# One load per weight, halves joined by fp32 products, and an earlier hidden layer in a decode kernel

The kernel runs on one core of a Trainium2 chip. The metric is device microseconds of one execution; quoted times are medians of several runs, and a ratio is the mean time of one kernel's fast runs over the mean of the other's fast runs in the same rounds, so it is not quite the ratio of the quoted medians. A run is called slow when it is over 1.5% above the fastest of the same kernel. Spans in a profile are about 1.8 us shorter than the time of the same run.

## The reference

Two blocks on the same normalized token, for a batch of 2: attention of one query over the last 2048 keys, and a feed-forward layer with squared ReLU; both are added to the input.

```python
xn = _layernorm(x)                                # x: 2 x 1 x 576
q = (xn @ wq)                                     # wq: 576 x 4096, 32 query heads of 128
scores = einsum("bhqd,bhkd->bhqk", q, k) * 128**-0.5    # 16 kv heads, 2048 keys
o = einsum("bhqk,bhkd->bhqd", softmax(scores), v)
A = o.reshape(B, 1, 4096) @ wo                    # wo: 4096 x 576
h = xn @ w1 + b1                                  # w1: 576 x 4608
B = relu(h)**2 @ w2 + b2                          # w2: 4608 x 576
return x + A + B
```

## The kernel before

The work on K and V is cut into 8 units u (4 kv heads of one sample), 2 MB of K and 2 MB of V each. `step(u)` transposes K of unit u, multiplies it with q, takes the softmax, and in its gaps multiplies the probabilities of unit u-2 with V. The loads stand in one queue in program order. These are the parts that the change touches:

```python
# weights: 4 whole rows per partition (512 of the 576 rows) in two loads, the remaining 64 rows in a third
def issue_w(tiles, wt, i, name, width, lrem):
    if i < NFULL // RW:
        tl = wbig.tile([P, RW * WBW], BF16, tag="wbig", name=f"{name}_{i}")        # two buffers
        ...
    else:
        tl = wrem.tile([P, WRW], BF16, tag="wrem", name=f"{name}_rem")
...
def pv_sum(u):                # sum of exp over partitions: one fp32 product with a 128x128 weight
    if u % (2 * B) == 0:
        sm_tiles[tq // 2] = psum.tile([P, B * Dh + 2 * B], F32, tag="sm", ...)       # one bank
    rs = sm_tiles[tq // 2][:, B * Dh + u % (2 * B):...]
    pe_mm(rs, lhsT=samec[:]..., rhs=sum_tiles.pop(u)[:], start=True, stop=True, ...)
    nc.vector.reciprocal(out=ri[:], in_=rs)
    nc.vector.tensor_scalar(out=f[:], in0=own_j[:], scalar1=ri[:, 0:1], ...)         # factors of o
...
def mlp_h_end():              # squared ReLU on rows, then nine bf16 transposes of every ninth column
    ...
    for r in range(FR):
        pe_tr(out=ha[:, r, 0:RB], in_=hrow[:, r:HW:FR], identity=ident[0:RB, 0:RB])
...
load_k(1); load_v(0); load_k(2); load_v(1); load_k(3)
...
step(1)
for u in range(2, NU - 1):
    step(u)
    ...
    if u == 4:
        issue_wo(0)
        for i in range(NW): issue_w1(i)           # w1 is loaded in the middle
    ...
pv_out(NU - 4); pv_all(NU - 3); wo_acc(0)
for c in range(KC): mlp_h_block(c)                # hidden layer in the tail, piece by piece
mlp_h_end()
pv_out(NU - 3)
step(NU - 1, with_pv=False)
pv_all(NU - 2); pv_out(NU - 2); pv_all(NU - 1); pv_out(NU - 1)
wo_acc(1)
for w in W2P[:NG4 - 1]: mlp_o(*w)                 # products with w2
```

Of the kernel before, what the change touches and what calls it, by code (L numbers as in the profile page):

```python
# [8 lines left out]
F32 = mybir.dt.float32  # L9
# [7 lines left out]
def kernel(  # L17
# [15 lines left out]
    P = 128  # L33
# [23 lines left out]
    NFULL = D // P  # L57
    RW = 2
    REM = D - NFULL * P
    S = P // REM  # L60
    KC = NFULL + 1
    NXN = NFULL + S
    LQ = (Hq * Dh) // S
    L1 = F // S
    NG4 = 4
    QW = Hq * Dh // NG4
    QB = QW // 2
    QH = QW // Dh
# [3 lines left out]
    RB = 32 * (NG4 - 1) + B  # L72
# [9 lines left out]
    wbig = ctx.enter_context(tc.tile_pool(name="wbig", bufs=NFULL // RW))  # L82
    wrem = ctx.enter_context(tc.tile_pool(name="wrem", bufs=1))
# [14 lines left out]
    k_tiles, v_tiles, wq_tiles, w1_tiles, wo_tiles, w2_tiles = {}, {}, {}, {}, {}, {}  # L98
    WBW = max(Hq * Dh, F)
    WRW = max(LQ, L1)  # L100
# [13 lines left out]
    def issue_w(tiles, wt, i, name, width, lrem):  # L114
        if i < NFULL // RW:
            tl = wbig.tile([P, RW * WBW], BF16, tag="wbig", name=f"{name}_{i}")
            rows = wt[0:NFULL * P, :].rearrange("(p r) n -> p (r n)", r=NFULL)
            nc.sync.dma_start(out=tl[:, 0:RW * width], in_=rows[:, i * RW * width:(i + 1) * RW * width])  # L118
            for r in range(RW):
                tiles[i * RW + r] = tl[:, r * width:(r + 1) * width]  # L120
        else:
            tl = wrem.tile([P, WRW], BF16, tag="wrem", name=f"{name}_rem")
            nc.sync.dma_start(out=tl[:, 0:lrem], in_=wt[NFULL * P:D, :].rearrange("r (s l) -> (r s) l", s=S))  # L123
            tiles[NFULL] = tl

    def issue_wq(c):
        issue_w(wq_tiles, A_wq, c, "wq", Hq * Dh, LQ)

    def issue_w1(c):
        issue_w(w1_tiles, B_w1, c, "w1", F, L1)  # L130

    def w_rows(tiles, c, col0, n, L):
        if c < NFULL:
            return tiles[c][:, col0:col0 + n], c
        sg = col0 // L
        assert (col0 + n - 1) // L == sg
        return tiles[c][:, col0 - sg * L:col0 - sg * L + n], NFULL + sg
# [20 lines left out]
    x_sb = const.tile([B, D], BF16, name="x_sb")  # L158
    nc.scalar.dma_start(out=x_sb[:], in_=x2d)
# [6 lines left out]
    NW = NFULL // RW + 1  # L166
    for i in range(NW):
        issue_wq(i)
    ones_f = const.tile([P, P], F32, name="ones_f")
    nc.vector.memset(ones_f[:], 1.0)  # L170
    col_f = const.tile([P, P], F32, name="col_f")
# [12 lines left out]
    ones_b = const.tile([1, B], BF16, name="ones_b")  # L184
    nc.vector.memset(ones_b[:], 1.0)
# [3 lines left out]
    for i in range(2):  # L189
        nc.vector.bn_stats(out=stats[:, i, :], in_=x_sb[:, i * half_d:(i + 1) * half_d])  # L190
# [6 lines left out]
    xn_sb = const.tile([B, D], BF16, name="xn_sb")  # L197
    nc.vector.tensor_scalar(out=xn_sb[:], in0=x_sb[:], scalar1=mv[:, 0:1], scalar2=rstd[:, 0:1],  # L198
                            op0=ALU.subtract, op1=ALU.mult)
    xr_sb = const.tile([B, S, P], BF16, name="xr_sb")  # L200
    nc.vector.memset(xr_sb[:], 0.0)
    for sg in range(S):
        nc.vector.tensor_copy(out=xr_sb[:, sg, sg::S], in_=xn_sb[:, NFULL * P:D])

    pro_ps = psum.tile([P, NXN, B], BF16, tag="misc", name="pro_ps")
    for c in range(NFULL):
        pe_tr(out=pro_ps[:, c, :], in_=xn_sb[:, c:NFULL * P:NFULL], identity=ident[:B, :B])
    for sg in range(S):
        pe_tr(out=pro_ps[:, NFULL + sg, :], in_=xr_sb[:, sg, :], identity=ident[:B, :B])
    xnT = const.tile([P, NXN, B], BF16, name="xnT")  # L210
    nc.vector.tensor_copy(out=xnT[:], in_=pro_ps[:])
# [21 lines left out]
    samec = const.tile([P, P // NC, NC], F32, name="samec")  # L233
    nc.gpsimd.tensor_copy(out=samec[:], in_=own[:].unsqueeze(1).to_broadcast([P, P // NC, NC]))
    tohead = const.tile([P, NC, DW], F32, name="tohead")
    nc.gpsimd.tensor_copy(out=tohead[:], in_=own[:].unsqueeze(2).to_broadcast([P, NC, DW]))
    qz = const.tile([P, 2, NU, 2, 4, NC], BF16, name="qz")
# [16 lines left out]
    def q_block(c):  # L254
        for k in range(2):
            for g in range(NG4):
                rhs, xc = w_rows(wq_tiles, c, g * QW + k * QB, QB, LQ)
                pe_mm(q_ps[k][32 * g:32 * g + B, :], lhsT=xnT[:, xc, :], rhs=rhs,
                                 start=(c == 0), stop=(c == KC - 1), skip_group_check=True,
                                 tile_position=(0, 32 * g))  # L260
        if c == KC - 1:
            qrow = const.tile([RB, QW], BF16, tag="row", name="qrow")
            nc.vector.tensor_copy(out=qrow[:, 0:QB], in_=q_ps[0][0:RB, :])
            nc.scalar.copy(out=qrow[:, QB:QW], in_=q_ps[1][0:RB, :])
            qT_ps = psum.tile([P, QH, P], BF16, tag="misc", name="qT_ps")
            for i in range(QH):
                pe_tr(out=qT_ps[:, i, 0:RB], in_=qrow[:, i * Dh:(i + 1) * Dh],
                                    identity=ident[0:RB, 0:RB])
            qT_v = qT_ps[:].rearrange("p i (g s) -> p i g s", s=32)
            for b in range(B):  # L270
                nc.vector.tensor_copy(out=qT_all[:, b, :].rearrange("p (g i) -> p i g", g=NG4), in_=qT_v[:, :, :, b])
            qe_ps = psum.tile([P, 2 * NU, NC], F32, tag="sm", name="qe_ps")
            for e in range(2):
                pe_mm(qe_ps[:, e * NU:(e + 1) * NU, :], lhsT=par[:, e, :, :].rearrange("p a i -> p (a i)"),
                                 rhs=qT_all[:].rearrange("p b h -> p (b h)"), start=True, stop=True)
            for a, cp in ((0, nc.vector.tensor_copy), (1, nc.scalar.copy)):
                lo, hi = a * (P // 2), (a + 1) * (P // 2)
                for w in range(2):
                    cp(out=qz[lo:hi, :, :, w, 2 * w + a, :].rearrange("p e u c -> p (e u) c"), in_=qe_ps[lo:hi, :, :])

    kT_tiles, sc_tiles, pT_tiles, sum_tiles, sm_tiles = {}, {}, {}, {}, {}
# [34 lines left out]
    def softmax(u):  # L316
# [12 lines left out]
        sums = keep.tile([P, 1], F32, tag="sums", name=f"sums_{u}")  # L329
        nc.scalar.activation(out=pr[:], in_=sc_ps, func=ACT.Exp, bias=nb[:], scale=scale, accum_out=sums[:])  # L330
        pT = keep.tile([P, NT, 32], BF16, tag="pT", name=f"pT_{u}")
        nc.vector.transpose(out=pT[:].rearrange("p t m -> p (t m)"), in_=pr[:])  # L332
        pT_tiles[u], sum_tiles[u] = pT, sums
# [3 lines left out]
    def pv_sum(u):  # L337
        tq, b = divmod(u, B)
        if u % (2 * B) == 0:
            sm_tiles[tq // 2] = psum.tile([P, B * Dh + 2 * B], F32, tag="sm", name=f"sm_{tq // 2}")  # L340
        rs = sm_tiles[tq // 2][:, B * Dh + u % (2 * B):B * Dh + u % (2 * B) + 1]
        pe_mm(rs, lhsT=samec[:].rearrange("p x c -> p (x c)"), rhs=sum_tiles.pop(u)[:],
                         start=True, stop=True, skip_group_check=True)
        f = work.tile([P, 4], F32, tag="f", name=f"f_{u}")
        ri = work.tile([P, 1], F32, tag="ri", name=f"ri_{u}")
        nc.vector.reciprocal(out=ri[:], in_=rs)
        nc.vector.tensor_scalar(out=f[:], in0=own_j[:], scalar1=ri[:, 0:1], scalar2=None, op0=ALU.mult)
        pv_cur[u] = (psum.tile([P, 4, Dh], F32, tag="misc", name=f"pv_ps_{u}"), f)

    def pv(u, i):  # L350
        pv_ps, f = pv_cur[u]
        v = v_tiles[u][:].rearrange("p (w t x) -> p t w x", w=2, t=NT)
        for k in range(4):
            t = 4 * i + k
            pe_mm(pv_ps[32 * k:32 * (k + 1), :, :].rearrange("m (w a) d -> m w (a d)", w=2),
                                  lhsT=pT_tiles[u][:, t, :], rhs=v[:, t, :, :], start=(i == 0),
                                  stop=(i == NT // 4 - 1), skip_group_check=True, tile_position=(0, 32 * k))

    def pv_mix(u):
        pv_ps, f = pv_cur[u]  # L360
        acc = None
        for j in range(4):
            nx = work.tile([P, Dh], F32, tag=f"acc{j % 2}", name=f"acc_{u}_{j}")
            if j == 0:
                op = nc.vector.tensor_scalar(out=nx[:], in0=pv_ps[:, j, :], scalar1=f[:, j:j + 1], scalar2=None,
                                             op0=ALU.mult)
            else:
                op = nc.vector.scalar_tensor_tensor(out=nx[:], in0=pv_ps[:, j, :], scalar=f[:, j:j + 1], in1=acc[:],  # L368
                                                    op0=ALU.mult, op1=ALU.add)
            tc.keep_in_program_order(op)  # L370
            acc = nx
        pv_cur[u] = acc
# [4 lines left out]
    def pv_out(u):  # L377
        tq, b = divmod(u, B)
        t, half = divmod(tq, 2)
# [204 lines left out]
```

## Time and profile before

| | before |
|---|---|
| median time | 134.56 us (134.39 to 134.71, 4 runs) |
| span of the profiled run | 132.7 us |
| TensorE busy; its granted clock, as a share of full clock | 90.6 us; 0.896 |
| last transfer packet ends | 128.9 us |

The page's head, its transfer row and the end of the timeline are in the prediction below. Further lines of the timeline of the kernel before (columns: start, duration, engine, line, operation, output and inputs, shapes, count, and in brackets the idle time ahead and what ended it):

```profile
35.09 1.09 PE L93 MATMUL kT_ps<-ident_f,k 128*128 128x128 f32 x8 [1.48 <-DMA k<-in_A_k_cache_dram]
...
78.39 0.58 PE L90 MATMUL sm<-sums,samec 128*128 128x1 f32 x2 [2.77 <-DVE od L386]
...
96.75 0.66 PE L90 MATMUL h_ps<-w_rem,xnT 128*2 128x384 bf16 x12 [0.22 <-DMA w_rem<-in_B_w_dram]
99.45 0.74 PE L93 MATMUL ha_ps<-ident,hrow 98*128 98x98 bf16 x9 [2.04 <-DVE hrow L421]
101.82 4.55 PE L93 MATMUL kT_ps<-ident_f,k 128*128 128x128 f32 x24 [1.27 <-DMA k<-in_A_k_cache_dram]
...
122.32 2.37 PE L90 MATMUL out_ps<-w,hT_sb 128*2 128x288 bf16 x36
126.20 1.27 PE L90 MATMUL out_ps<-w,hT_sb 128*2 128x288 bf16 x18 [1.51 <-DMA w<-in_B_w_dram]
```

Step 2 starts when K2 lands (35.1), step 7 when K7 lands (101.8), and the products with w2 wait for w2 (126.2). At each of these places TensorE waits for a transfer, so lateness that arose in between is forgiven. Of the waits that are not for a transfer, one is 2.8 us at 78 us, where the softmax sum of a new half needs the one bank (a part of the memory that TensorE writes) that `od` still has to read.

### The profile page before, as it was taken

To read this page: it belongs to the slowest core of one execution; us is meant where nothing else is said; L and a number is where in the kernel's file an instruction comes from. 1 tells how busy PE (TensorE), PEld (TensorE's weight loads), DVE (VectorE), ACT (ScalarE), POOL (GpSimd) and SP (SyncE) were. 2 spreads that over 40 slices of the span, in tenths; PEclk is the share of its full clock that TensorE was granted. 3 is DMA by queue.
4 is the path that set the end of the run, shared out by engine and by line. 5 is a ranking of instruction groups with operands and counts; after the bars stand their busy time and mean duration, and the time that the engine had idled before them with its cause. 6 is when DMAs were issued, how large, how long until landed. Compare 5 with 4: busy or idle time off the path is not lost.

```text
span 132.7 us, 2075 instructions
## 1 busy us (share of the span) xinstructions
PE 90.6 (68%) x846; PEld 54.2 (41%) x846; DVE 61.5 (46%) x169; ACT 46.2 (35%) x63; POOL 7.3 (6%) x20
## 2 busy tenths in 40 slices
PE   0059645986599689688788639959736974549561
PEld 0059312553356355454444325526315931225330
DVE  6914404264552872873763772277141447540021
ACT  6705502196343274175175133332040752000001
POOL 7500000100100100100100100001000001000000
PEclk9999995599959999999999975799998699855999
DMA  4999999999999999999999999999999999999950
GB/s 154 400 403 444 420 440 430 435 430 415 442 420 435 425 435 425 430 439 425 439 420 444 417 432 422 438 444 439 412 420 425 435 433 433 413 428 433 415 210 1
DMA packets 4260, 53.74 MB, mean 405 GB/s; under 512 B 530, under 2 KB 536, under 8 KB 1052
## 3 DMA queue, kind: packets, MB, share of 16 engines
q1 hardware_dynamic: 4180, 53.61, 95.1%
q8 instruction: 6, 0.10, 0.3%
q0 software_dynamic: 64, 0.01, 0.0%
q14 instruction: 2, 0.02, 0.0%
q10 hardware_dynamic: 8, 0.00, 0.0%
HBM read 53.62 MB, written 0.00 MB: 404 GB/s over the span
## 4 chain that ended last, share of the span: by engine, by line
DMA 73%; PE 13%; SPq 4%; DVE 3%; issue 2%; ACT 2%; POOL 1%; ACTq 0%; POOLq 0%
DMA w_rem<-in_B_w_dram 26%; DMA w<-in_B_w_dram 24%; DMA k<-in_A_k_cache_dram 23%; PE kT_ps L93 8%; PE pv_ps L90 2%; PE sc_ps L90 2%; SPq L118 1%; ACT kT L297 1%; SPq L111 1%; DVE kT L299 1%; DVE mx L319 1%; PE tail_ps L90 1%; POOL gmax L323 1%; SPq L142 0%; SPq L123 0%
## 5 line engine op out<-in xcount | busy, mean ns | idle before, releaser
L93 PE MATMUL kT_ps<-ident_f,k 128*128 128x128 f32 x256 | 43.3, 318 | 7.0 <-DMA k<-in_A_k_cache_dram 4.9
L297 ACT COPY kT<-kT_ps 128x1024 bf16<-128x1024 bf16 x32 | 31.8, 1012 | 31.7 <-PE kT_ps L93 31.6
L93 PEld LDWEIGHTS kT_ps<-ident_f,k 128*128 128x128 f32 x256 | 33.4, 163 | 20.2 <-issue 7.6
L299 DVE COPY kT<-kT_ps 128x1024 bf16<-128x1024 bf16 x32 | 21.9, 685 | 30.8 <-PE kT_ps L93 30.8
L90 PE MATMUL sc_ps<-kT,qz 128*32 128x512 bf16 x128 | 10.5, 413 | 6.5 <-DVE kT L299 5.5
L330 ACT ACTIVATE pr<-sc_ps,nb 128x512 bf16<-128x512 f32 x8 | 5.5, 687 | 20.3 <-DVE nb L327 20.3
L90 PE MATMUL pv_ps<-v,pT 128*32 128x512 bf16 x128 | 12.4, 428 | 0.0
L323 POOL PARTITION_ALL_REDUCE gmax<-m x8 | 2.9, 364 | 102.1 <-DVE m L321 81.2
L368 DVE SCALAR_TENSOR_TENSOR acc<-pv_ps,f,acc 128x128 f32<-128x128 f32 x24 | 8.3, 346 | 0.5
L332 DVE STREAM_TRANSPOSE pT<-pr 128x512 bf16<-128x512 bf16 x8 | 5.7, 709 | 4.8 <-ACT pr L330 4.8
L90 PE MATMUL sm<-acc,tohead 128*64 128x128 f32 x16 | 3.7, 315 | 5.7 <-DVE acc L368 5.5
L319 DVE TENSOR_REDUCE mx<-sc_ps 128x1 f32<-128x512 f32 x8 | 5.5, 691 | 4.2 <-PE sc_ps L90 3.8
L90 PE MATMUL out_ps<-wo,ws 128*2 128x288 bf16 x64 | 5.9, 356 | 1.1 <-DVE ws L390 1.1
L90 PEld LDWEIGHTS <-qz 128*32 128x32 bf16 x128 | 2.2, 98 | 10.8 <-DVE kT L299 7.1
L552 ACT CAST fin_sb<-tail_ps 2x144 bf16<-2x144 f32 x2 | 0.5, 272 | 17.5 <-PE tail_ps L90 17.4
L90 PE MATMUL sm<-sums,samec 128*128 128x1 f32 x16 | 3.2, 267 | 2.8 <-DVE od L386 2.8
L90 PEld LDWEIGHTS <-xnT 128*2 128x2 bf16 x100 | 2.4, 82 | 6.5 <-issue 5.0
L541 DVE COPY part<-out_ps 2x288 f32<-2x288 f32 x2 | 0.9, 448 | 8.9 <-PE out_ps L90 8.9
L90 PEld LDWEIGHTS sm<-acc,tohead 128*64 128x64 f32 x16 | 1.6, 143 | 8.1 <-DVE acc L368 7.5
L93 PE MATMUL pro_ps<-ident,xn_sb 2*128 2x2 bf16 x4 | 0.3, 172 | 6.7 <-DVE xn_sb L198 6.7
L90 PEld LDWEIGHTS <-ws 128*2 128x2 bf16 x64 | 3.3, 102 | 3.8 <-DVE ws L390 1.5
L90 PEld LDWEIGHTS <-pT 128*32 128x32 bf16 x128 | 3.1, 95 | 4.1 <-issue 3.3
(86 smaller groups left out, 64.1 us busy)
## 6 DMA issues: line engine op xcount, KB each, us to landing
k<-in_A_k_cache_dram SPq DMA_DIRECT2D x8, 2048.0 KB, 21.8
v<-in_A_v_cache_dram SPq DMA_DIRECT2D x8, 2048.0 KB, 26.6
wo<-in_A_wo_dram SPq DMA_DIRECT2D x2, 2304.0 KB, 23.4
w<-in_B_w_dram SPq DMA_DIRECT2D x2, 2304.0 KB, 30.9
wq<-in_A_wq_dram SPq DMA_DIRECT2D x2, 2048.0 KB, 13.8
w<-in_B_w_dram SPq DMA_DIRECT2D x3, 1296.0 KB, 28.7
w<-in_B_w_dram SPq DMA_DIRECT2D x1, 1008.0 KB, 31.8
w_rem<-in_B_w_dram SPq DMA_DIRECT2D x1, 576.0 KB, 34.3
```

The costliest lines, as they stand in the source:

```text
L90: return tc.keep_in_program_order(nc.tensor.matmul(out, **kw))
L93: return tc.keep_in_program_order(nc.tensor.transpose(**kw))
L111: return [lambda i=i: nc.sync.dma_start(out=tl[:, i * n:(i + 1) * n], in_=v[:, :, i * n:(i + 1) * n]) for i in range(parts)]
L118: nc.sync.dma_start(out=tl[:, 0:RW * width], in_=rows[:, i * RW * width:(i + 1) * RW * width])
L297: nc.scalar.copy(out=dst, in_=src)
L299: nc.vector.tensor_copy(out=dst, in_=src)
L319: nc.vector.tensor_reduce(out=mx[:], in_=sc_ps, axis=AX.X, op=ALU.max)
L323: nc.gpsimd.partition_all_reduce(gmax[:], m2[:], channels=P, reduce_op=ReduceOp.max)
L330: nc.scalar.activation(out=pr[:], in_=sc_ps, func=ACT.Exp, bias=nb[:], scale=scale, accum_out=sums[:])
L332: nc.vector.transpose(out=pT[:].rearrange("p t m -> p (t m)"), in_=pr[:])
L368: op = nc.vector.scalar_tensor_tensor(out=nx[:], in0=pv_ps[:, j, :], scalar=f[:, j:j + 1], in1=acc[:], op0=ALU.mult, op1=ALU.add)
L541: nc.vector.tensor_copy(out=part[:, i * OH:(i + 1) * OH], in_=out_ps[32 * i:32 * i + B, :])
```

## The change

Each of wq and w1 is to come as one load with 4.5 rows, that is nine half rows, in every partition. A half row can be the left or the right half of a weight row, so a product yields four rows (two samples, two halves), and the halves that belong together are added by a product with a 0/1 selector, in fp32 so that the halves are not rounded to bf16 first. w1 is loaded ahead of K2 and its products stand between steps 1 and 2, so that the tail is relieved. The sum of exp rides as a 129th column in the o product.

```diff
-    wbig = ctx.enter_context(tc.tile_pool(name="wbig", bufs=NFULL // RW))
-    wrem = ctx.enter_context(tc.tile_pool(name="wrem", bufs=1))
+    wbig = ctx.enter_context(tc.tile_pool(name="wbig", bufs=1))
...
+    def issue_w(wt, name, width):
+        tl = wbig.tile([P, HP * FL], BF16, tag="wbig", name=f"{name}_sb")
+        nc.sync.dma_start(out=tl[:, 0:HP * width], in_=wt.rearrange("d (s l) -> (d s) l", s=2)
+                          .rearrange("(p r) l -> p (r l)", r=HP))
...
-        sums = keep.tile([P, 1], F32, tag="sums", name=f"sums_{u}")
+        acc = keep.tile([P, Dh + 1], F32, tag="acc", bufs=4, name=f"acc_{u}")
...                      # pv_sum (a product, a reciprocal, a scaling per unit) goes
-                         lhsT=tohead[:]..., rhs=pv_cur.pop(u)[:], ...
+                         lhsT=tohead[:]..., rhs=acc_tiles.pop(u)[:], ...     # 129 columns
...
     def mlp_h_end():
-        ...pe_tr(out=ha[:, r, 0:RB], in_=hrow[:, r:HW:FR], identity=ident[0:RB, 0:RB])
+        hrow = const.tile([RB, HW], F32, tag="row", name="hrow")
+        for k in range(3):
+            nc.scalar.copy(out=hrow[:, k * HB:(k + 1) * HB], in_=mlp["ps"][k][0:RB, :])
+        for r in range(FR):
+            pe_mm(hT_ps[:, r, :], lhsT=hrow[:, r:HW:FR], rhs=sel_h[0:RB, :, :]..., start=True, stop=True)
...
     load_v(0)
+    issue_w(B_w1, "w1", FL)
     load_k(2)
...
     step(1)
+    mlp_h_start()
+    mlp_h_all()
+    mlp_h_end()
     load_k(4)
...
-    for c in range(KC):
-        mlp_h_block(c)
-    mlp_h_end()
```

The same is done for q, and b1 and b2 are loaded from ACT's queue.

## The prediction

> **What bounds the kernel now.** I read the page's head and its slices first, to see which resource is full and when; then the table of DMA queues, then the stretches of a few microseconds, then the order of the loads on their queue, then the timeline of the last six microseconds.
>
> ```profile
> span 132.7 us, 2075 instructions
> DMA  4999999999999999999999999999999999999950
> GB/s 154 400 403 444 420 440 430 435 430 415 442 420 435 425 435 425 430 439 425 439 420 444 417 432 422 438 444 439 412 420 425 435 433 433 413 428 433 415 210 1
> q1 hardware_dynamic: 4180, 53.61, 95.1%
> DMA 73%; PE 13%; SPq 4%; DVE 3%; issue 2%; ACT 2%; POOL 1%; ACTq 0%; POOLq 0%
> ```
>
> The row DMA is 9 from the second slice to the 38th: the sixteen transfer engines have no hole. One queue moves 53.61 MB and its packets fill 95.1% of 132.7 us, that is 126.2 us per engine. The chain that ended last is 73% transfer. PE, the busiest compute engine, is at 68%. In the stretches (columns: busy times, granted clock, DMA share, GB/s):
>
> ```profile
> 26.00:76.00 50.00, 40.37 (x334) 23.66 (x332) 28.78 (x72) 24.55 (x32) 2.19 (x6) 0.96 1.01 430
> 76.00:96.00 20.00, 15.01 (x154) 8.29 (x158) 9.35 (x24) 5.41 (x8) 0.36 (x1) 0.83 1.00 427
> 110.00:126.00 16.00, 9.36 (x106) 4.82 (x105) 5.75 (x19) 0.78 (x2) 0.36 (x1) 0.79 1.00 424
> ```
>
> The share is 1.00 or more wherever I cut: K and V (first row), wo and w1 (second), w2 (third). So the time is about 2.1 us before the first packet, 126 to 127 us of uninterrupted packets, and a tail. The tail, from the timeline:
>
> ```profile
> 127.50 0.93 DVE L541 COPY part<-out_ps 2x288 f32<-2x288 f32 x2 [8.86 <-PE out_ps L90]
> 128.64 0.61 PE L90 MATMUL tail_ps<-w,hT_sb 128*2 128x144 bf16 x28 [1.17 <-DMA w<-in_B_w_dram]
> 129.53 0.29 PE L90 MATMUL tail_ps<-w,hT_sb 128*2 128x144 bf16 x8
> 130.50 0.33 SPq L553 DMA_DIRECT2D out_dram<-fin_sb  x1
> ```
>
> The last products wait for w2, and 4.1 us follow. Nothing in the change touches that code.
>
> The trace's packet records give a price list. Medians: 16,384 bytes 611 ns, 18,432 bytes 686, 10,368 bytes 389, 8,064 bytes 305, 4,608 bytes 178, 4,096 bytes 159, 2,304 bytes 93; a completion write 9 ns. From 16,384 and 4,096: (611 - 159)/12,288 = 0.0368 ns a byte, 27.2 GB/s per engine or 435 GB/s for sixteen, and 159 - 151 = 8.4 ns fixed per packet. The first packet of K0 starts at 2.13 us, the last of w2 ends at 128.9.
>
> **What the skill says.** The Trainium skill, "DMA: Bandwidth & Descriptors", section "Where 436 GB/s comes from", puts the ceiling of sixteen ports at 435.2 GB/s: the trace agrees, its slope is 435 and its plateau 424 to 431. The same page, "Why small descriptors are slow (HBM only)", has a fixed overhead per packet of about 3 cycles, with examples near 256 bytes; the trace shows 8.4 ns, 1.4% of a 16 KB packet. The same page, "Issuing engines are not separate DMA queues", says loads from another engine's queue save only issue time; in this trace SP's queue carries all but a few KB, so moving b1 and b2 to ACT buys no bandwidth. "TensorE: Matmul & The Clock Gate", Part 1, has TensorE at half clock after about 3.4 us without work; the trace agrees, granted 0.50 at 20 to 26 us after the wait for wq. I use it where the new block of products follows a wait.
>
> **The change, part by part.**
>
> Bytes: unchanged, 53.6 MB.
>
> Packets. K, V, wo and w2 are untouched. wq was 256 packets of 16,384 and 128 of 4,096; on one engine, 16 x 611 + 8 x 159 = 11.05 us. Now 128 rows of 9 x 2048 x 2 = 36,864 bytes; if each is one packet (18,432 bytes are one packet now), the estimate is 8 x (36,864 x 0.0368 + 8.4) = 10.92. w1 was 16 x 686 + 8 x 178 = 12.40; now 8 rows of 41,472 bytes, estimate 8 x (1,526 + 8.4) = 12.28. Four loads fewer save four completion writes, 0.04. Sum: 0.13 + 0.12 + 0.04 = **0.3 us off every transfer engine**, all of it on the path that sets the end.
>
> Start. ACT issues four small loads more behind x, at 0.54 us each as x's issue took: its Sqrt, the layernorm and the first transposes come some 2 us later (xnT was written at 7.2). But wq lands only at about 19 us and K0's transposes have from 8.5 until then, with 5.4 us of work; PE sits idle from 15.8 to 18.0 today. Hidden. K0's own issue is first on SP as before: 0 to 0.1 us.
>
> q. Today the last product comes 0.65 us after the last piece of wq. Now all 36 products wait for the one load: 36 x 64 ns (16 took 1.03 us) = 2.3 us, 4.6 at half clock. Eight fp32 products replace eight transposes (0.83 us); an fp32 product is about 0.2 us each in the pair sm<-acc,tohead (2 in 0.43), so 1.6 us. Scores of unit 0 start 2.5 to 5 us later than 23.1. This is in the shade of transfers.
>
> MLP. With 4.90 us for a 2 MB load, the transfer times are: K0 to 7.0, wq to 18.0, K1 22.9, V0 27.8, w1 40.0, K2 44.9, V1 49.8, K3 54.7, V2 59.6, K4 64.5. w1 in hand at about 41, 54 products at 49 ns (24 took 1.15 us) are 2.6 us, 5.3 at half clock; copies of h by ACT about 1.4; nine fp32 products about 2. K2's transposes start at 47 to 50 instead of 35.1. The block leaves the stretch 93 to 101 us.
>
> Softmax sums. Eight fp32 products with a loaded 128x128 weight go (3.2 us of PE, "sm<-sums,samec", eight times 0.38) and with them eight reciprocals and eight scalings (0.15 + 0.23 us of DVE). A column is added to the o product. About 0.4 us per unit of PE, and the 2.8 us wait of sm on od at 75 to 78 us; none of it on the transfers' path.
>
> Total: 134.62 - 0.3 + 0.05 = **134.3 us**.
>
> **Rivals.**
>
> *A hole in the transfers because w1 has to wait for wq's buffer.* There is now one large weight buffer; w1's issue must wait for the last q product, and SP's queue is in order, so K2 waits behind it. Outstanding then: K1 and V0, until 27.8 us. The q products end at 21.5 to 24, the issue needs under 1 us more. 3 to 5 us of slack: no hole, but it is the narrowest place. If q were done only at 30 us it would cost 2 to 3 us: 137.
>
> *A later PE starves the K/V buffers.* Steps run at 9.7 us today (K5 issued at 43.35, K6 at 53.03: these are releases by consecutive steps) against 9.8 for a K and a V. Starting step 2 at 50, V0's buffer comes free at about 56.5 and V3 is wanted at 64.5; K2's at 59 for K5 at 69.4; K5's at 88 for V7 at 104. Every slack is over 7 us, and wo's 5.5 us give more. If steps slowed to 11 us it would begin to bite: 135 to 137. Against it: each step loses 0.4 us of work.
>
> *The long packets are better or worse than the line.* At the asymptote the whole stream cannot be faster than 53.61/0.435 = 123.2 us, 3 us under today's, and only two of 26 big loads change form, so better is worth the 0.3 and no more. If 36 KB rows are cut back to 16 KB pieces by the hardware, the gain is nearer 0.1. If they ran 5% slower: 23.2 x 0.05 = +1.2, so 135.5.
>
> *The slowest engine.* An undisturbed engine would end at 2.13 + 125.4 = 127.6; the slowest ends at 128.9. Six 16 KB instruction fetches of about 0.9 us fall on single transfer engines. The change keeps PE's instruction count within some ten, so I expect six again, but which engines they hit may move the end by 0.5 us either way.
>
> **Range and chances.** The sum moves 0.3 us; placement of the fetches gives 0.5, the long packets up to 1. So 133.5 to 135.1. Faster by 2% means 131.9: more than nine times the packet saving, against the unchanged bytes: 3%. Slower by 2% (137.3) needs a hole of 3 us, from one of the first two rivals: 3%. Within 2%: 94%.
>
> **What would show it.** After: q1 with about 450 to 500 fewer packets and the same 53.6 MB; the DMA row again 9 throughout; no dip around 25 to 30 us (w1 after V0); w1 landing near 41, h products there and none near 93; K2's transposes near 48; "sm<-sums" gone; w2's last landing within 0.5 us of 128.6 and 4.1 us after it. A dip of the DMA row anywhere, a wait of SP for q_ps that outlasts V0, or a final landing earlier than 127.5 would make the prediction wrong.

## The result, and the profile after

The changed kernel takes 138.82 us (138.42 to 139.07, 4 runs); the ratio is 1.0314, 95% interval 1.0286 to 1.0342. It is 4.3 us slower, outside the predicted range. From its page:

```profile
span 137.1 us, 2051 instructions
DMA  4999999999979999999999999999999999999300
q1 hardware_dynamic: 3604, 53.61, 92.1%
PE 42%; DMA 28%; DVE 15%; ACT 7%; issue 4%; POOL 1%; SPq 0%; POOLq 0%; ACTq 0%
```

The transfers did what was expected: no hole, the same bytes, 576 packets fewer, the last packet at 129.4 us instead of 128.9. The 7 in the DMA row is no hole: by the packets' own starts and ends, the sixteen engines are busy in full in every microsecond from 26 to 48; the long packets of w1 are only booked unevenly to the slices (520 GB/s in one, 323 in the next). But the chain that ended last, 73% transfers before, is now 42% TensorE and 28% transfers. The time after the last packet grew from 3.8 to 7.7 us. The timeline of the changed kernel, TensorE, ACT's copies and the last issue:

```profile
43.33 4.49 PE L84 MATMUL h_ps<-w_sb,xnT 128*4 128x384 bf16 x54 [4.87 <-DMA w_sb<-in_B_w_dram]
47.58 1.24 ACT L414 COPY hrow<-h_ps 100x384 f32<-100x384 f32 x3 [6.98 <-PE h_ps L84]
48.88 4.46 PE L84 MATMUL hT_ps<-sel_h,hrow 100*128 100x8 f32 x18 [1.06 <-ACT hrow L414]
53.19 1.95 PE L87 MATMUL kT_ps<-ident_f,k 128*128 128x128 f32 x8
...
107.26 1.53 PE L87 MATMUL kT_ps<-ident_f,k 128*128 128x128 f32 x12
...
125.35 3.94 PE L84 MATMUL out_ps<-wo,ws 128*2 128x288 bf16 x32 [1.52 <-DVE ws L382]
129.13 3.23 PE L84 MATMUL out_ps<-w,hT_sb 128*2 128x288 bf16 x50
...
134.94 0.33 SPq L539 DMA_DIRECT2D out_dram<-fin_sb  x1
```

Step 2 starts at 53.2 instead of 35.1, without a bracket: K2 had landed at 48.1 (the last of its sixteen completion writes) and waited. Steps 3 to 6 follow every 9.67 us (K loads that each wait for the release of a step's buffer are issued at 61.70, 71.38 and 81.05), step 7 starts at 107.3 instead of 101.8, and the first products with w2 start at 129.1, 50 in one row, when nearly all of w2 is there. None of the waits for K7 and w2 that forgave lateness before is left.

### The profile page after: what moved, and what is told of

The parts are those of the page before. It is cut to its first block, busy times and chain, and to the rows that moved or that the text cites. A ratio compares the mean times of both kernels' runs of the same rounds, so it can differ in the third digit from the quotient of the medians.

```text
span 137.1 us, 2051 instructions
## 1 busy us (share of the span) xinstructions
PE 93.7 (68%) x839; PEld 56.5 (41%) x839; DVE 58.2 (42%) x147; ACT 43.7 (32%) x62; POOL 8.1 (6%) x28
## 4 chain that ended last, share of the span: by engine, by line
PE 42%; DMA 28%; DVE 15%; ACT 7%; issue 4%; POOL 1%; SPq 0%; POOLq 0%; ACTq 0%
PE kT_ps L87 15%; DMA w_sb<-in_B_w_dram 14%; DMA wq_sb<-in_A_wq_dram 14%; PE sc_ps L84 7%; PE out_ps L84 5%; PE pv_ps L84 5%; ACT kT L289 3%; PE hT_ps L84 3%; DVE kT L291 3%; PE h_ps L84 3%; DVE mx L311 3%; PE q_ps L84 3%; DVE mix L353 3%; ACT pr L322 2%; POOL gmax L315 1%
## 5 line engine op out<-in xcount | busy, mean ns | idle before, releaser
L87 PE MATMUL kT_ps<-ident_f,k 128*128 128x128 f32 x256 | 41.5, 310 | 4.4 <-ACT kT L289 3.4
L87 PEld LDWEIGHTS kT_ps<-ident_f,k 128*128 128x128 f32 x256 | 32.5, 159 | 15.7 <-issue 8.7
L84 PE MATMUL sm<-acc,tohead 128*64 128x129 f32 x16 | 4.0, 334 | 9.1 <-DVE acc L353 9.1
L84 PEld LDWEIGHTS <-xnT 128*4 128x4 bf16 x90 | 3.1, 118 | 14.9 <-issue 14.8
L84 PE MATMUL h_ps<-w_sb,xnT 128*4 128x384 bf16 x54 | 4.5, 501 | 4.9 <-DMA w_sb<-in_B_w_dram 4.9
L84 PE MATMUL q_ps<-wq_sb,xnT 128*4 128x512 bf16 x36 | 3.7, 589 | 5.3 <-DMA wq_sb<-in_A_wq_dram 5.3
L353 DVE SCALAR_TENSOR_TENSOR mix<-pv_ps,own_j,mix 128x128 f32<-128x128 f32 x16 | 5.6, 348 | 0.4
L87 PE MATMUL pro_ps<-ident,xs 2*128 2x2 bf16 x10 | 0.6, 165 | 7.0 <-DVE xs L179 7.0
```

Source lines behind the costliest of these rows:

```text
L84: return tc.keep_in_program_order(nc.tensor.matmul(out, **kw))
L87: return tc.keep_in_program_order(nc.tensor.transpose(**kw))
L353: op = nc.vector.scalar_tensor_tensor(out=nx, in0=pv_ps[:, j, :], scalar=own_j[:, j:j + 1], in1=acc, op0=ALU.mult, op1=ALU.add)
```

## The experiments

All were run beside the kernel before, and the ratios are to it. Theory and rival are in the expectations; several were wrong.

| run | what it is | median us | ratio |
|---|---|---|---|
| a1_both_late | changed, w1 and its products late again | 141.42 and 140.11 (the two fast runs) | 1.0459 |
| a2_products_late | changed, only the products late | 142.05 | 1.0565 |
| a3_bf16_join | changed, joins in bf16 | 134.82 | 1.0030 |
| a4_warm | changed, clock kept up ahead of w1 | 137.96 | 1.0252 |
| c1_contig_join | changed, fp32 joins without stride | 135.25 | 1.0035 |
| b1_before_early | before, order alone changed | 138.23 | 1.0250 (1.0199 to 1.0301: slower, but unclear whether by 2%) |
| b2_k2_first | changed, K2 ahead of w1 | 135.01 | 1.0019 |
| b3_tail_order | changed, tail reordered | 134.76 | 1.0015 |
| c2_late_bf16 | a1 with bf16 joins | 135.07 | 1.0052 |
| e1_before_early_sums | b1 with the new sums | 134.38 | 0.9994 |
| e2_old_sums | changed, with the old sums | 142.31 | 1.0584 |
| d1_bf16_tail | a3 and b3 together | 135.30 | 1.0051 |

### Is it the order?

```diff
 a1:  -    issue_w(B_w1, "w1", FL)                  # ahead of K2
      -    mlp_h_start(); mlp_h_all(); mlp_h_end()  # after step(1)
      +            issue_w(B_w1, "w1", FL)          # after issue_wo(0), in the loop
      +    mlp_h_start()                            # after the loads of w2
      +    mlp_h_all(); mlp_h_end()                 # after wo_acc(0), in the tail
 a2:  the same without moving the load
```

> The changed kernel with w1 loaded where the kernel before loads it (behind wo of the first half) and the hidden-layer products in the tail as before; the single large loads, the fp32 joins and the sums in the o product stay. Theory (order): the loss is that K2 lands 12 us later and the compute chain of units 2 to 7, which repeats every 9.67 us, has no slack to make that up; with the order undone the time is set by transfers again: 134.3, at most 135.5 if the slower fp32 joins in the tail show. Rival (joins): if the single loads or fp32 joins cost by themselves, it stays at 137 or more.

> The changed kernel with w1 still loaded ahead of K2, but the hidden-layer products in the tail, where the kernel before has them. Theory (order of loads): step 2 starts at 48 when K2 lands, 5 us earlier than 53.2, but the tail gets a block of 6 to 7 us at full clock; the chain is still the bound, so no gain: 138.5 to 140.5. Rival (place of the products): if the products between steps 1 and 2 are the cause, moving them away brings it back to 134 to 135.

a1 took 141.42 and 140.11 us in its fast runs, some 2 us more than the changed kernel (1.0459 against 1.0314), and a2 142.05, also above what was expected. The first theory, that the order alone is to blame, fell with a1: the order of the change is a gain for its own new parts. The timeline of a1 shows what those parts do in the tail:

```profile
97.69 4.75 PE L84 MATMUL h_ps<-w_sb,xnT 128*4 128x384 bf16 x54 [5.01 <-DMA w_sb<-in_B_w_dram]
103.34 4.47 PE L84 MATMUL hT_ps<-sel_h,hrow 100*128 100x8 f32 x18 [0.91 <-ACT hrow L414]
...
108.36 4.75 PE L87 MATMUL kT_ps<-ident_f,k 128*128 128x128 f32 x24
```

With one load nothing of w1 can be multiplied until all of it is there: the products start at 97.7, when those of the kernel before were finished (96.75 + 0.66), and at half clock. Then come the joins with 4.5 us.

### Is it the joins?

```diff
 a3: -        hrow = const.tile([RB, HW], F32, ...)     and sel_h in F32
     +        hrow = const.tile([RB, HW], BF16, ...)    and sel_h in BF16
 c1: -            pe_mm(..., lhsT=hrow[:, r:HW:FR], ...)
     +            pe_mm(..., lhsT=hrow[:, r * P:(r + 1) * P], ...)
 a4: +    for i in range(22):
     +        pe_mm(fill[:], lhsT=ident[:], rhs=v_tiles[0][:, 0:4 * Dh], start=True, stop=True, ...)
          mlp_h_all()
```

> The changed kernel with the row of h halves and its selector in bf16 instead of fp32, so nine single-pass products join the halves in place of nine fp32 ones (18 records, 4.46 us at half clock). The halves are rounded before they are summed, so the result is a little less exact. Theory (order, chain without slack): whatever shortens the block ahead of step 2 comes off the end one for one: about 1.3 us for the joins instead of 4.5, so step 2 at 50 and the time at 135.7, 3.1 us less. Rival (the joins are not on the path): unchanged, 138.8.

> The changed kernel with 22 idle products of 512 columns while TensorE waits for w1, so that its clock is still granted in full when w1 lands; they write a bank that nobody reads. Theory: h products 2.7 instead of 4.5 us and joins 2.3 instead of 4.5, step 2 at 49.3, and the same amount off the end: 134.9, or the floor of the transfers, 134.3. Rival (the clock does not matter there): 138.8, or more if the fill runs into w1.

> The changed kernel, its joins still in fp32, but each reads 128 neighbouring columns of the row instead of every ninth. The hidden units come out permuted, so the result is wrong on purpose; number and shape of the instructions are the same. Theory (the weight loads of the joins are slow because of their stride: 336 ns each at every clock, against 192 ns for the contiguous ones of q): the joins take 2.2 us instead of 4.46, step 2 starts at 51, the time falls to 136 to 136.6. Rival (fp32 itself is slow there): 138.8 again.

a3 is correct and takes 134.82 us: nearly the whole loss is gone (ratio 1.0030, 1.0007 to 1.0053). Its timeline:

```profile
48.79 0.73 PE L84 MATMUL hT_ps<-sel_h,hrow 100*128 100x8 bf16 x9 [0.82 <-ACT hrow L414]
49.38 1.07 PE L87 MATMUL kT_ps<-ident_f,k 128*128 128x128 f32 x8
...
126.37 1.27 PE L84 MATMUL out_ps<-w,hT_sb 128*2 128x288 bf16 x18 [0.60 <-DMA w<-in_B_w_dram]
128.81 0.61 PE L84 MATMUL tail_ps<-w,hT_sb 128*2 128x144 bf16 x28 [1.18 <-DMA w<-in_B_w_dram]
```

The joins take 0.73 instead of 4.46 us, step 2 starts 3.8 us earlier, and its first eight transposes take 1.07 instead of 1.95 us: in the changed kernel the clock was at half after the joins (0.50 from 53.2 to 55.0), in a3 at full (1.00 from 49.4 to 50.4). The products with w2 wait for w2 again, so the time is the transfers' once more.

c1 took 135.25 us and keeps fp32: its joins take 2.17 us, as expected. Its output is wrong, which doesn't matter for the time.

```profile
48.15 2.17 PE L84 MATMUL hT_ps<-sel_h,hrow 100*128 100x8 f32 x18 [0.30 <-ACT hrow L414]
50.18 1.71 PE L87 MATMUL kT_ps<-ident_f,k 128*128 128x128 f32 x8
```

The time is 0.75 us below the range that I had expected. The cost lies in the stride. Weight loads (columns: minimum, median and maximum ns, then first and last start in us) of the changed kernel, for the joins of h with a step of nine columns and for those of q without:

```profile
L84 PEld LDWEIGHTS hT_ps<-sel_h,hrow x18: 313/336/338, 48.9 to 52.9; 100*128 100x128 f32 x18
```

```profile
L84 PEld LDWEIGHTS qs_ps<-sel_q,qrow x16: 186/192/192, 24.6 to 26.3; 100*128 100x128 f32 x16
```

The loads overlap, so the joins' pace is the distance of the starts: 0.24 us with the step (48.9 to 52.9 for 18), 0.11 us without.

a4 took 137.96 us, 0.9 us less than the changed kernel where I expected 3.9. The fill kept the clock up and shortened the h products from 4.49 to 2.60 us, but ran on 2 us past the landing of w1, and the joins did not care. In this profiled run, the slowest of a4's four, the fill began 2 us late because q's joins ran at half clock, 3.56 us instead of 1.93; the edit does not reach so far back. First the timeline of a4, then its stretches during and after the joins (clock, transfer share and GB/s are the last three columns):

```profile
45.45 2.60 PE L85 MATMUL h_ps<-w_sb,xnT 128*4 128x384 bf16 x54
49.12 4.47 PE L85 MATMUL hT_ps<-sel_h,hrow 100*128 100x8 f32 x18 [1.06 <-ACT hrow L415]
53.44 1.95 PE L88 MATMUL kT_ps<-ident_f,k 128*128 128x128 f32 x8
```

```profile
49.12:51.30 2.18, 2.18 (x10) 2.18 (x10) 0.00 (x0) 0.00 (x0) 0.00 (x0) 1.00 1.03 436
51.30:53.50 2.20, 2.20 (x11) 2.20 (x12) 0.00 (x0) 0.00 (x0) 0.00 (x0) 0.94 0.96 410
53.50:55.30 1.80, 1.80 (x9) 1.48 (x8) 0.23 (x1) 0.91 (x2) 0.00 (x0) 0.50 1.02 437
```

4.47 us at a clock of 1.00 to 0.94 and 4.46 at about 0.7: weight loads fill these joins (2.18 of 2.18 us), and their pace does not follow the clock. That of loads without the step does; q's in a4, at a clock of 0.50, start 0.21 us apart instead of 0.11:

```profile
L85 PEld LDWEIGHTS qs_ps<-sel_q,qrow x16: 286/333/333, 24.9 to 28.0; 100*128 100x128 f32 x16
```

And although TensorE shows busy throughout the joins, the granted clock fell to 0.50 at their end, with no idle time but the 1.06 us ahead of them.

### The order alone, and the sums

```diff
 b1 (to the kernel before):
     load_k(1); load_v(0)
 +   for i in range(NW): issue_w1(i)
 ...
     step(1)
 +   mlp_h_start(); (all mlp_h_block); mlp_h_end()      # gone from the tail
 e1: b1 with softmax, pv_start, pv_mix and pv_out of the changed kernel
 e2: the changed kernel with softmax, pv_sum, pv_mix and pv_out of the kernel before
```

> The kernel before with nothing but the order changed: w1, still in three loads, ahead of K2, and the hidden layer's products and bf16 transposes between steps 1 and 2. Theory (the order alone is harmless as long as the block is done when K2 lands at about 48): the first pieces of w1 land early and are multiplied on arrival, the last lands near 42, the block ends by 47, step 2 starts at 48, the time is the transfers': 134.6, at most 135.2. Rival (order alone is the cause, K2 being 12 us later): 137.5 or more.

b1 took 138.23 us where I expected 134.6, though its block did end in time and step 2 started at 47.7. The timeline shows where it lost:

```profile
47.72 1.94 PE L93 MATMUL kT_ps<-ident_f,k 128*128 128x128 f32 x8
...
92.36 0.59 PE L90 MATMUL sm<-sums,samec 128*128 128x1 f32 x2 [2.77 <-DVE od L386]
...
107.78 1.53 PE L93 MATMUL kT_ps<-ident_f,k 128*128 128x128 f32 x12
```

It is the wait of the old softmax sum, and the clock then was at 0.50 from 92 to 96. In the kernel before the same wait lies ahead of a transfer that TensorE must wait for anyway.

> b1_before_early (the kernel before with w1 and its products early) with the softmax sums carried in the o product as in the change. Theory (in b1 step 2 started in time, at 47.7, and the loss came later, in the step of unit 6, where the first product of the next half waits 2.8 us for od to read the one bank and the clock then falls to half): that wait goes, step 7 starts at about 103 instead of 107.8, and the time is the transfers': 134.5 to 135.2. Rival (K2's lateness itself): 138 again.

> The changed kernel with the old softmax sums, a product and two small DVE operations per unit, everything else as changed. Theory (the sums in the o product are a gain on a chain that is now the bound: 2.8 us of wait in the step of unit 6 and some 2 us of half clock behind it): 142.5 to 144. Rival (the sums are hidden, as I predicted): 138.8 to 139.3.

e1 took 134.38 us, ratio 0.9994 (0.9978 to 1.0011), and e2 142.31. Both theories held, with both times 0.1 to 0.2 us below their ranges. In e1 the wait is gone, and TensorE waits for w2 again:

```profile
88.32 0.43 PE L90 MATMUL sm<-acc,tohead 128*64 128x129 f32 x2 [0.42 <-DVE acc L359]
...
128.54 0.61 PE L90 MATMUL tail_ps<-w,hT_sb 128*2 128x144 bf16 x28 [1.07 <-DMA w<-in_B_w_dram]
```

By the ratios the same order costs 3.4 us with the old sums and nothing with the new ones, and without the new sums the change would have lost 7.8 us instead of 4.3. e1 is the kernel before with two parts of the change and without the single loads and joins; it is as fast as the kernel before, not faster.

### Where the slack lies

```diff
 b2: -    issue_w(B_w1, "w1", FL); load_k(2)      products after step(1)
     +    load_k(2); issue_w(B_w1, "w1", FL)      products after step(2)
 b3: -    pv_all(NU - 1); pv_out(NU - 1); wo_acc(1); mlp_o(*W2P[0]); mlp_o(*W2P[1]); mlp_o(*W2P[2])
     +    pv_all(NU - 1); mlp_o(*W2P[0]); pv_out(NU - 1); mlp_o(*W2P[1]); wo_acc(1); mlp_o(*W2P[2])
 c2: a1 and a3 together.   d1: a3 and b3 together.
```

> The changed kernel with K2 loaded ahead of w1 and the hidden layer's products after step 2 instead of before it; slow fp32 joins and single loads stay. Theory (only what is on the chain behind the last K matters): step 2 from 38 to 48, the block from 48 to about 57 while K3 lands near 57, steps 3 to 6 as late as in the kernel before or little more, and the time is the transfers': 134.4 to 135.0. Rival (the block costs its length wherever it stands): 138 or more.

> The changed kernel with the order of the tail alone changed: the products with the first three pieces of w2, which need nothing of the attention, go into TensorE's waits for the last o products instead of behind them. Theory (the end is TensorE's chain, not the transfers): 3.2 us of products leave the end and the clock is granted for longer, so 135 to 136. Rival (the end is set by the last landing of w2): 138.8 again.

b2 took 135.01 us: the slow joins may stand as they are if a step's worth of work is done while w1 comes. b3 took 134.76, below the 135 to 136 expected: the late chain may stand as it is if the products with w2 go into its gaps. Its timeline ends on the transfers again:

```profile
128.74 0.61 PE L84 MATMUL tail_ps<-w,hT_sb 128*2 128x144 bf16 x28 [0.43 <-DMA w<-in_B_w_dram]
```

> The changed kernel with w1 and its products back in the order of the kernel before (as in a1_both_late) and with bf16 joins (as in a3_bf16_join): single loads and the sums in the o product are what is left of the change. Theory (the single load of w1 costs by itself where its products stand behind it: 54 products start only when the last byte is there, at half clock, 5 us later than with three loads): 4 us less than a1_both_late, 137.5 to 138.5. Rival (only the joins were slow): 134.5 to 135.2.

c2 took 135.07 us; I had expected 137.5 to 138.5. So what is left of the change in the old order, the single loads, bf16 joins and new sums together, costs about 0.7 us against the kernel before (ratio 1.0052, 1.0012 to 1.0093), though the products with w1 end 5 us later: the slack takes up most of it. Of the 6.2 us that a1's fast runs lost, the fp32 joins made nearly all: in the two profiles (141.42 and 136.0 us) the first score product of step 7 comes at 113.05 in a1 and 107.62 in c2, 5.4 us apart, 3.8 of it the joins themselves (4.47 against 0.70) and the rest mostly transposes at half clock behind them.

> The changed kernel with both repairs, bf16 joins and the w2 products in the waits of the tail. Theory (each repair alone reached the transfers' floor, so both together gain nothing more): 134.4 to 134.9, with TensorE waiting for the last pieces of w2. Rival (there is still chain on the path): 133.5 to 134.2.

d1 took 135.30 us in the median, but its profiled run 134.54, with TensorE waiting for w2. The other three runs, 135.1 to 135.6, have no trace; what held them up is open. The profile has one warning: bf16 joins alone do not keep the clock up. In d1 it was at 0.50 before, during and after them, and the first transposes took as long as in the changed kernel:

```profile
48.78 0.71 PE L84 MATMUL hT_ps<-sel_h,hrow 100*128 100x8 bf16 x9 [0.75 <-ACT hrow L414]
49.34 1.95 PE L87 MATMUL kT_ps<-ident_f,k 128*128 128x128 f32 x8
```

No version here beats the kernel before beyond noise.

## Why the prediction was wrong

**The bound, the bytes and the transfers: right, with no gain from the packets.** No hole came, w1 behind q did not starve the queue, and the long packets lie on the predicted line (medians 1,364 and 1,533 ns; predicted 1,364 and 1,534). The 0.3 us did not come: the packets of an engine still add up to 126.2 us. Single long packets took up to 2.4 us, and the means, 1,394 and 1,549 ns, ate the saving. The count of packets fell by 576, not by "about 450 to 500": the prediction's own list gives 512 packets and 64 completion writes. (Its total, 134.62 - 0.3 + 0.05, is 134.37 and not 134.3; nothing hangs on it.)

**The step that failed: "nine fp32 products about 2", and with it "K2's transposes start at 47 to 50".** The joins took 4.46 us. I took their price from sm<-acc,tohead (0.43 us for two instructions, one fp32 product), and counted even that wrongly as two products; neither the stride of nine nor the two instructions of every fp32 product was in the sum. c1 shows the stride to make 2.3 us of it. Without the stride nine products take 2.17 us there, so the wrong count did no harm, by luck. w1 also came 2.3 us later than 41, because its slowest engine ends at 42.8 where I had reckoned with an undisturbed one. Step 2 started at 53.2. In a3 and c1 it started inside the predicted 47 to 50 or just behind it, at 49.4 and 50.2, and the times, 134.82 and 135.25, lie within the predicted range or 0.15 us above it.

**What the joins did beyond themselves.** The clock fell to 0.50 while they ran or as they ended, in the changed kernel (1.00 at 48.9 to 50, 0.50 from 51) and in every other profile with fp32 joins of step nine; d1 shows that it can also be low there without them. From the start of the joins' copies to the first score product of step 2 the changed kernel is 5.7 us behind a3 (59.72 against 54.05 us), 3.7 of it the joins (4.46 - 0.73) and the rest nearly all transposes at the lower clock. a3 ends on the transfers with little room, the changed kernel ends 4.3 us later, so about 1.4 us of the 5.7 were slack, an estimate from these two profiled runs.

**The rival that came true was tested with the wrong measure.** "A later PE starves the K/V buffers" was written down and dismissed because every buffer had over 7 us. The buffers did have it. What was not asked is when the chain itself ends if step 2 starts at 50: five steps of 9.67 us, step 7 and the tail have only some 1.4 us to spare, by the estimate above, once w1 is ahead of K2, and unlike in the kernel before, no later transfer makes them wait and forgives lateness. b3 shows that the end is this chain and not the buffers, b2 that the slack lies on the other side of K2.

**The sums: "none of it on the transfers' path" fits the kernel before, where no run changes them alone, and was wrong for the changed one.** By the ratios, taking them into the o product is worth 3.6 us there (e2 against the changed kernel) and 3.4 us in b1 against e1, by the 2.8 us wait and the half clock behind it. "About 0.4 us per unit" did not show in the pace: 9.68 us a step before (issues at 43.35 and 53.03), 9.67 after.

**q: right in its effect.** Its joins took 1.93 us, and TensorE still waited 4.87 us for w1 afterwards.

**A reading that does not hold.** "The trace agrees" on half clock after about 3.4 us without work says too much: TensorE's wait for wq, ahead of the 0.50 at 20 to 26 us, was 2.25 us (15.78 to 18.03).

## What to carry to other kernels

Where a kernel sits on its transfers, look for the places where compute waits for a load and count what has to fit between two of them; a change of order can take such a place away, and then every microsecond of the chain counts, though nothing of it did before. Check both questions: when the buffers come free, and when the chain itself ends. Price an instruction from a row with the same element type, shape and stride, or measure it by itself first.

## What the Trainium skill lacked or had wrong

- "TensorE: Matmul & The Clock Gate", section "LDWEIGHTS (loading the stationary operand)", gives the time of a weight load by its columns alone, about columns / 1.2 ns, some 107 ns for 128. Since loads overlap in the traces, the pace of their starts is what compares with it, here for 128 columns: 0.11 us for fp32 without a step at full clock agrees; 0.21 us at a clock of 0.50 (a4), 0.24 us for fp32 with a step of nine at either clock, and 0.06 us for bf16 with the step of nine (a3, 48.8 to 49.3 for nine) do not. The section "Weight-path perf modes" of that page does have faster loads for types other than fp32, and "SBUF — State Buffer" a penalty for strides that leave a 16-byte line. What no page has is a figure for a strided fp32 weight load, or that it did not follow the clock.
- The same page, Part 1, ties the fall to half clock to idle windows of about 3.4 us. In a4 the clock fell to 0.50 at the end of 4.5 us of fp32 products with eight moving columns, during which TensorE shows no idle time (1.06 us ahead of them); in the kernel before, 0.50 followed a wait of only 2.25 us. Which activity the monitor counts was not tested here.
- No page has the price of packets above 16 KB: 36,864 bytes took 1,364 ns and 41,472 bytes 1,533 ns in the median, on one line with the shorter ones.
